# Eight PSUM banks, shared out anew while only attention runs: five for the scores and two for the transposes instead of three and four

## The chip, the cores and the metric

The kernel runs on one core of a Trainium2 chip. The core has a matrix engine (TensorE, PE in the rows below; its weight loads are shown apart as PEld), a vector engine (DVE), a scalar engine (ACT), a general engine (POOL) and a queue that only issues transfers (SP). Each engine works through its own list of instructions in the order in which it was emitted and waits where an operand or a buffer isn't ready. Matrix results go to PSUM, which has eight banks of 128 x 512 float32; DVE and ACT read them there. The metric is the device time of one execution in microseconds (us), as the median of several runs.

## What is computed

Attention with pooled queries, then two MLPs one after the other, on 4 batches, 8 heads, 1152 keys, 576 pooled queries and a head width of 64; then 2304 tokens with a model width of 512 and 2048 hidden units.

```python
q_pool = q.reshape(B, H, S // 2, 2, D).mean(axis=3)
scores = scale * np.matmul(q_pool, k.transpose(0, 1, 3, 2))
scores = scores - np.max(scores, axis=-1, keepdims=True)
attn = np.exp(scores)
attn = attn / (np.sum(attn, axis=-1, keepdims=True) + 1e-09)
x = heads_to_columns(np.matmul(attn, v))                  # [2304, 512]
h = x @ w_in;  x = np.maximum(0.01 * h, h) @ w_out        # first MLP
h = x @ w_in2; g = np.where(h > 0.0, h, np.exp(np.minimum(h, 0.0)) - 1.0)
out = g @ w_out2
```

## The kernel before

Every large product is carried in pieces: a float32 value is split into h (rounded) and l (the rest), and the product is the sum of three, or of two with h stacked over l.

Attention goes by pairs of heads: 4 batches of 4 pairs, 16 pairs in all. A pair has nine tiles of 128 queries. For one tile:

- `scores` (L438): three score matmul groups of 384 keys, each into a PSUM bank of its own (L452, two or four matmuls), the maximum of each bank on DVE (L457), the maximum of the three (L459, DVE), and then three exponentials on ACT (L463), which read the same three banks again and write P to SBUF. A score bank is free only after its exponential.
- `transpose_p` (L469): P goes through PE again in three groups of three 128 x 128 transposes, each group into a PSUM bank (L475). ACT copies the bank out as h (L261), DVE subtracts to get l (L267), and then the bank is free.
- `pv` (L489): P times V into the one bank `o` (L496), added up on ACT (L507) and DVE (L509).

Each pair also has transposes of its keys (`kn`) and queries (`qn`, `qxn`) into PSUM (L373), copied out by ACT (L386, L409, L418). At its end `normalise` (L513) transposes the reciprocal sums twice (L535, L542), and DVE multiplies out of these two banks (L538, L546). A pair ends with L538.

The MLPs take a batch at a time (L629 up, L667 down), and begin as soon as a batch's four pairs are normalised. So the first four pairs, those of batch 0, run with no MLP beside them; after that an MLP always does. What runs beside the first four pairs on DVE, ACT and POOL is the conversion of MLP weights (`ct`, `cr`, `cm`, `wr`, L293 to L305), as far as there are buffers for it.

The eight banks have names: three `s`, two `t`, one `o`, two `h`. `h` is the MLPs' pair. While the first four pairs are emitted (`first_window`), a table EARLY lends `h` to attention: `pbank` (L432) deals out the banks of a use in the order that the table's string spells.

The order of the instructions of each engine is made by a list scheduler in the kernel (`Program`, L37), from costs in the code, ranks, and the rule that a bank's next use waits for all readers of its last. A change of the banks therefore gives every engine another order.

Of the kernel before, what the change touches and what calls it, by code (L numbers as in the profile page):

```python
# [18 lines left out]
class Buf:  # L19
    """A tile that is allocated when the first operation on it is emitted."""  # L20
# [16 lines left out]
class Program:  # L37
    """Operations in the order of the computation, emitted in the order in which a
    list schedule by their costs (ns) and ranks starts them.

    A tile's k-th use of a tag waits for its (k - bufs)-th to be through."""
# [15 lines left out]
    def add(self, engine, cost, rank, fn, w=(), r=()):  # L57
        """fn() emits; w and r name the tiles (or (tile, part)) written and read."""
        me = len(self.ops)
        deps, starts, frees = set(), set(), []  # L60
# [4 lines left out]
        for x in r:  # L65
            b, part = x if isinstance(x, tuple) else (x, None)
# [88 lines left out]
def kernel(  # L155
# [11 lines left out]
    """Pooled-query attention, then a leaky-max MLP, then an ELU MLP.  # L167

    Every float32 operand of a large product is carried as h + l, h being the
    value rounded to float32r and l the exact rest (also a float32r); products  # L170
    sum h*h + h*l + l*h. Contractions of 64 stack h over l on 128 partitions.
    Tokens of a batch are kept in columns (t, p) -> row 4 p + t for the first
    512 and in order for the last 64; the output stores undo that.
    """
# [6 lines left out]
    NQ = S // 2  # L181
# [30 lines left out]
    EARLY = {'s': 'sss', 't': 'tthh'}  # L212
# [36 lines left out]
    def act(n, accum=False, sbuf=False):  # L249
        return 50 + 0.833 * n + (190 if accum else 0) + (43 if sbuf else 0)  # L250
# [7 lines left out]
    def psplit(rank, h, l, hi, lo, src, n, w, r, w_l=None, fast=True, psum=False):  # L258
        """hi = round(src) on engine h, lo = src - hi on engine l (AP makers)."""
# [11 lines left out]
    def convert(rank, dst, src):  # L271
        """dst = src, a [128, 512] block of weights, as float32; float64 comes as its bits.

        With e the 11 exponent bits, a float32's exponent is e's top bit and its
        low seven while 897 <= e <= 1150; below that the value is a zero. The
        mantissa's last 29 bits are rounded and added to the rest as integers.
        """
# [33 lines left out]
    def load_w(rank, layer, w_in, w_out, f):  # L311
        """h and l of the f-th 128 hidden units' columns of w_in and rows of w_out."""
# [456 lines left out]
```

## Time and profile before

| | us |
|---|---|
| median of 3 runs (lowest, highest) | 1550.54 (1548.72, 1550.97) |
| span of the profiled execution | 1550.8 |
| PE busy in it | 1421.8 (92%) |
| DVE busy | 1093.0 (70%) |
| ACT busy | 1027.4 (66%) |
| POOL busy | 844.7 (54%) |

The profiled execution's span is 0.3 us above the median of the runs and within their spread. Busy times are of the whole span; the stages differ much, so the rows below give them for stretches.

### The profile page before, as it was taken

How to read it: one execution, taken by the hardware profiler on the slowest of the kernel's cores; microseconds unless marked ns; L12 is line 12 of the kernel's file. 1: busy time of each engine (PE TensorE's matmuls, PEld its weight loads, DVE VectorE, ACT ScalarE, POOL GpSimd, SP SyncE). 2: the span in 40 equal slices, each digit the busy share in tenths (PEclk: the TensorE clock that was granted, in tenths of full speed). 3: DMA queues.
4: the chain of work that ended last, by engine and by line, in shares of the span. 5: the costliest groups of instructions: out<-in, count | busy, mean ns of one | idle time of the engine just before them, and what ended most of it. 6: DMA issues, size and time to landing. Idle time of an engine off the chain costs nothing.

```text
span 1550.8 us, 28885 instructions
## 1 busy us (share of the span) xinstructions
PE 1421.8 (92%) x10288; PEld 1368.2 (88%) x10288; DVE 1093.0 (70%) x2401; ACT 1027.4 (66%) x2773; POOL 844.7 (54%) x840
## 2 busy tenths in 40 slices
PE   5878899889888888999999999999999998899998
PEld 5777788878777788999999998999999998899897
DVE  6998898989999999656676767556676664224333
ACT  6998888777677777676667766776667652442442
POOL 5444256666666667444455556454554445566572
PEclk9999999999999999999999999999999999999999
DMA  4232124433334443222222222222221111322230
GB/s 145 90 114 86 40 79 139 128 114 124 125 119 136 142 133 115 83 77 60 69 74 70 79 77 63 93 73 61 70 71 42 55 55 56 92 76 82 69 89 31
DMA packets 82641, 135.58 MB, mean 87 GB/s; under 512 B 8512, under 2 KB 26944, under 8 KB 82496
## 3 DMA queue, kind: packets, MB, share of 16 engines
q1 hardware_dynamic: 82496, 133.73, 28.4%
q8 instruction: 81, 1.33, 0.4%
q14 instruction: 64, 0.52, 0.1%
HBM read 112.20 MB, written 21.50 MB: 86 GB/s over the span
## 4 chain that ended last, share of the span: by engine, by line
PE 50%; DVE 13%; ACT 3%; issue 2%; DMA 2%; POOL 2%; SPq 0%; ACTq 0%; POOLq 0%; DVEq 0%
PE h L667 15%; PE h L629 12%; PE s L452 5%; PE o L496 5%; PE t L475 4%; PE s L629 2%; DVE t L648 2%; PE s L667 2%; PE t L629 2%; DVE wr L305 2%; PE t L667 2%; DVE t L651 1%; PE t L373 1%; DVE pt L267 1%; DVE m L457 1%
## 5 line engine op out<-in xcount | busy, mean ns | idle before, releaser
L667 PE MATMUL h<-g,wo 128*128 128x288 f32 x2544 | 442.1, 305 | 18.5 <-DVE t L651 10.8
L629 PE MATMUL h<-xs,wi 128*128 128x288 f32 x2520 | 428.2, 305 | 22.9 <-DVE t L651 9.7
L629 PEld LDWEIGHTS h<-xs,wi 128*128 128x128 f32 x2520 | 362.8, 191 | 35.7 <-DVE t L651 15.4
L667 PEld LDWEIGHTS h<-g,wo 128*128 128x128 f32 x2544 | 368.6, 190 | 23.9 <-DVE t L651 13.0
L457 DVE TENSOR_REDUCE m<-s 128x1 f32<-128x384 f32 x432 | 231.3, 550 | 53.0 <-PE s L452 50.0
L267 POOL TENSOR_TENSOR g<-t,g 128x288 fp32r<-128x288 f32 x256 | 218.9, 863 | 89.3 <-ACT g L261 85.6
L261 ACT ACTIVATE pt<-t 128x384 fp32r<-128x384 f32 (+1 forms) x416 | 183.0, 455 | 126.1 <-PE t L475 116.4
L463 ACT ACTIVATE p<-s,m 128x384 f32<-128x384 f32 x432 | 248.4, 585 | 23.1 <-DVE m L459 22.7
L267 DVE TENSOR_TENSOR pt<-t,pt 128x384 fp32r<-128x384 f32 (+1 forms) x416 | 206.1, 508 | 56.6 <-ACT pt L261 55.0
L267 POOL TENSOR_TENSOR wo<-wr,wo 128x512 fp32r<-128x512 f32 x128 | 168.3, 1321 | 136.0 <-ACT wo L261 126.9
L452 PE MATMUL s<-kT,qT 128*128 128x384 f32 x768 | 195.2, 353 | 27.9 <-ACT p L463 27.6
L267 POOL TENSOR_TENSOR wi<-wr,wi 128x512 fp32r<-128x512 f32 x128 | 171.4, 1339 | 62.4 <-ACT wi L261 50.6
L475 PE MATMUL t<-ident,p 128*128 128x128 f32 x1116 | 181.1, 276 | 19.4 <-DVE pt L267 13.2
L496 PE MATMUL o<-pt,vn 128*128 128x256 f32 (+1 forms) x1152 | 190.7, 301 | 4.4 <-DVE pt L267 2.5
L496 PEld LDWEIGHTS o<-pt,vn 128*128 128x128 f32 x1152 | 164.4, 189 | 8.4 <-DVE pt L267 5.6
L261 ACT ACTIVATE g<-t 128x288 fp32r<-128x288 f32 x256 | 112.7, 446 | 88.1 <-DVE t L651 50.0
L475 PEld LDWEIGHTS t<-ident,p 128*128 128x128 f32 x1116 | 137.9, 142 | 31.5 <-DVE pt L267 14.1
L642 DVE SCALAR_TENSOR_TENSOR t<-t 128x288 f32<-128x288 f32 x128 | 90.6, 714 | 97.1 <-ACT t L640 96.6
L303 POOL TENSOR_TENSOR ct<-ct,cr 128x256 uint32<-128x256 uint32 x128 | 98.8, 773 | 109.5 <-DVE ct L296 41.0
L452 PEld LDWEIGHTS s<-kT,qT 128*128 128x128 f32 x768 | 126.1, 192 | 35.9 <-ACT p L463 34.5
L267 POOL TENSOR_TENSOR vn<-raw,vn 128x576 fp32r<-128x576 f32 x32 | 45.9, 1436 | 166.2 <-ACT vn L261 166.2
L261 ACT ACTIVATE wo<-wr 128x512 fp32r<-128x512 f32 x128 | 80.3, 630 | 83.0 <-PE h L667 51.8
(104 smaller groups left out, 2091.6 us busy)
## 6 DMA issues: line engine op xcount, KB each, us to landing
wr<-w SPq DMA_DIRECT2D x192, 256.0 KB, 2.7
cr<-in_moe_w_in_dram SPq DMA_DIRECT2D x64, 256.0 KB, 2.7
cr<-in_moe_w_out_dram SPq DMA_DIRECT2D x64, 256.0 KB, 2.7
w<-wr SPq DMA_DIRECT2D x64, 256.0 KB, 2.1
raw<-in_k_dram SPq DMA_DIRECT2D x32, 288.0 KB, 3.1
raw<-in_v_dram SPq DMA_DIRECT2D x32, 288.0 KB, 3.0
raw<-in_q_dram SPq DMA_DIRECT2D x32, 256.0 KB, 3.0
out_dram<-cr SPq DMA_DIRECT2D x16, 256.0 KB, 2.2
```

The lines of the kernel that those rows point to most:

```text
L261: prog.add("ACT", act(n, sbuf=not psum), rank, lambda: A.activation(out=hi(), in_=src(), func=ACTF.Copy), w=[w], r=r)
L267: lambda: eng.tensor_tensor(out=lo(), in0=src(), in1=f32(hi()), op=ALU.subtract),
L303: prog.add("POOL", pool(CW), rank, lambda t=t, r=r: G.tensor_tensor(out=t.ap, in0=t.ap, in1=r[:, :, 0], op=ALU.add), w=[t], r=[t, (r, 0)])
L305: prog.add("DVE", dve(CW), rank, lambda n=n, t=t, mag=mag: V.scalar_tensor_tensor(out=dst[:, n:n + CW], in0=mag.ap, scalar=MIN_HI, in1=t.a ...
L452: PE.matmul(out=st[:, 0:384], lhsT=qa(a), rhs=kT[:, 384 * c:384 * c + 384], start=(i == 0), stop=(i == len(seq) - 1))
L457: prog.add("DVE", dve(384), rank - LR, lambda st=st, c=c: V.tensor_reduce(out=m[:, c:c + 1], in_=st[:, 0:384], axis=AX.X, op=ALU.max), w=[ ...
L463: prog.add("ACT", act(384, True), rank - LE, lambda c=c: A.activation(out=p[:, 384 * c:384 * c + 384], in_=banks[c][:, 0:384], func=ACTF.E ...
L475: PE.transpose(out=t[:, i, :], in_=p[:, (3 * c + i) * 128:(3 * c + i + 1) * 128], identity=ident)
L496: PE.matmul(out=o[:, 0:n], lhsT=vn[:, c, :], rhs=pt[th][:, a, c % 3, :], start=(c == 3 * ORDER[0] and a == 0), stop=(c == 3 * ORDER[2] + 2 ...
L629: PE.matmul(out=h[:, 0:HB], lhsT=wi[:, a, c, :], rhs=xs[c][:, e, cols], start=(c == 0 and a == 0 and e == 0), stop=(c == DC - 1 and a == 1))
L642: prog.add("DVE", dve(HB), rk, lambda t=t, g32=g32: V.scalar_tensor_tensor(out=g32.ap, in0=t.ap, scalar=0.01, in1=t.ap, op0=ALU.mult, op1= ...
L667: PE.matmul(out=y[:, 0:HB], lhsT=w[f][1][:, a, d * 128:(d + 1) * 128], rhs=g[f][:, e, cols], start=(f % FC == 0 and a == 0 and e == 0), st ...
```

## The change

The table's two strings are exchanged in their sense: the scores rotate over five banks (three `s`, then two `h`), and all transposes, of P, of keys and queries and of the reciprocal sums, keep the two `t` alone. Nothing else in the code changes (the diff also drops docstrings and comments, which aren't shown).

```diff
     SBUFS = 3
     RAWB = 3
-    EARLY = {'s': 'sss', 't': 'tthh'}
+    EARLY = {'s': 'ssshh', 't': 'tt'}
     T1B = 3
     HBUFS = 2
```

How PE's order changes from the third pair to the fourth, beginning with the normalisation of the third (`rb`: its reciprocal sums, `p`: P of a tile, `kn` and `qn`: keys and queries of the fourth pair's second head; the bank is named ahead of the arrow). Before:

```order
L452 MATMUL s<-kT,qT 128x384 x6
L535 MATMUL h<-ident,rb 128x128 x4
L542 MATMUL t<-ident,rb 128x128
L475 MATMUL t<-ident,p 128x128 x3
L475 MATMUL h<-ident,p 128x128 x6
L452 MATMUL s<-kT,qT 128x384 x4
L373 MATMUL t<-identr,kn 128x128 x6
L373 MATMUL h<-identr,kn 128x128 x3
L452 MATMUL s<-kT,qT 128x384 x2
L373 MATMUL h<-identr,qn 128x128 x4
L373 MATMUL t<-identr,qn 128x128 x4
L475 MATMUL t<-ident,p 128x128 x3
```

After the change, at the same place:

```order
L535 MATMUL t<-ident,rb 128x128 x4
L542 MATMUL t<-ident,rb 128x128
L452 MATMUL s<-kT,qT 128x384 x4
L475 MATMUL t<-ident,p 128x128 x9
L373 MATMUL t<-identr,kn 128x128 x3
L452 MATMUL s<-kT,qT 128x384 x2
L373 MATMUL t<-identr,kn 128x128 x6
L373 MATMUL t<-identr,qn 128x128 x8
L475 MATMUL t<-ident,p 128x128 x9
```

Thirteen groups of transposes in a row (two of `rb`, three of `p`, three of `kn`, two of `qn`, three of `p`) now share two banks, where four took them in turn; six score matmuls stand among them in both.

PE's order inside the fourth pair, from the transposes of the tile that mixes two heads (its scores are those with `rem`). Before:

```order
L475 MATMUL t<-ident,p 128x128 x6
L475 MATMUL h<-ident,p 128x128 x3
L452 MATMUL s<-kT,qT 128x384 x2
L475 MATMUL h<-ident,p 128x128 x3
L452 MATMUL s<-kT,qT 128x384 x2
L475 MATMUL t<-ident,p 128x128 x3
L452 MATMUL s<-kT,qT 128x384 x2
L475 MATMUL t<-ident,p 128x128 x3
L496 MATMUL o<-pt,vn 128x320 x12
```

After:

```order
L475 MATMUL t<-ident,p 128x128 x6
L452 MATMUL s<-kT,qT 128x384 x4
L475 MATMUL t<-ident,p 128x128 x3
L452 MATMUL h<-kT,qT 128x384 x2
L475 MATMUL t<-ident,p 128x128 x3
L452 MATMUL h<-kT,qT 128x384 x2
L452 MATMUL s<-kT,qT 128x384 x2
L475 MATMUL t<-ident,p 128x128 x6
L452 MATMUL s<-kT,qT 128x384 x2
```

Six groups of scores, two tiles, now stand where three stood, and they have moved ahead of transposes that they followed.

DVE's order up to the end of the fourth pair (L538). Before:

```order
L457 TENSOR_REDUCE m<-s 128x1 x3
L509 TENSOR_TENSOR xu<-o,tm 64x256
L459 TENSOR_REDUCE m<-m 128x1
L538 TENSOR_TENSOR xu<-h,xu 128x512
L267 TENSOR_TENSOR pt<-t,pt 128x3x128
```

After:

```order
L457 TENSOR_REDUCE m<-s 128x1
L459 TENSOR_REDUCE m<-m 128x1
L457 TENSOR_REDUCE m<-s 128x1
L509 TENSOR_TENSOR xu<-o,tm 64x256
L457 TENSOR_REDUCE m<-s 128x1
L538 TENSOR_TENSOR xu<-t,xu 128x512
L457 TENSOR_REDUCE m<-s 128x1
```

Two maxima of the next tile have moved ahead of L538; counted over the whole list, 116 maxima stand ahead of it instead of 114, and at the ends of the three pairs before it 37, 64 and 91 instead of 33, 60 and 87. The weight conversions ahead of the third and the fourth L538 are the same number as before. On PE, 18 matmuls of the first MLP (L629) now stand ahead of the fourth L535, where there were none. From the 3621st PE instruction on, of 10290, the order of PE is that of before.

## Rows read from the trace of the kernel before

**Rows 1.** The page's first lines: span, then busy us, share of the span and instructions of each engine.

```profile
span 1550.8 us, 28885 instructions
PE 1421.8 (92%) x10288; PEld 1368.2 (88%) x10288; DVE 1093.0 (70%) x2401; ACT 1027.4 (66%) x2773; POOL 844.7 (54%) x840
```

**Rows 2.** The end of each of the first four pairs: the four instructions of L538 on DVE (start us, length us, what).

```profile
67.33 0.69 DVE L538 TENSOR_TENSOR xu<-h,xu 128x512 f32<-128x512 f32 x1
113.62 0.69 DVE L538 TENSOR_TENSOR xu<-h,xu 128x512 f32<-128x512 f32 x1
159.14 0.69 DVE L538 TENSOR_TENSOR xu<-h,xu 128x512 f32<-128x512 f32 x1
201.93 0.69 DVE L538 TENSOR_TENSOR xu<-h,xu 128x512 f32<-128x512 f32 x1
```

**Rows 3.** Busy time by stretch: the first four pairs, then the stretch up to 620 us, then the rest (stretch, its length, busy us and instructions of each engine, granted clock, DMA share, GB/s).

```profile
0.00:67.33 67.33, 45.43 (x289) 40.80 (x289) 53.62 (x127) 52.42 (x145) 33.23 (x42) 1.00 0.43 131
67.33:113.62 46.29, 37.27 (x254) 33.73 (x254) 43.16 (x107) 42.15 (x123) 21.27 (x23) 0.96 0.31 97
113.62:159.14 45.52, 37.11 (x254) 33.90 (x254) 40.54 (x102) 40.51 (x118) 18.54 (x19) 0.96 0.27 86
159.14:201.93 42.79, 35.77 (x257) 32.90 (x258) 35.81 (x86) 36.15 (x104) 12.04 (x13) 1.00 0.14 42
201.93:620.00 418.07, 363.45 (x2553) 339.60 (x2552) 390.31 (x842) 311.06 (x863) 273.64 (x283) 0.98 0.40 124
620.00:1551.00 931.00, 902.81 (x6685) 887.23 (x6683) 529.58 (x1138) 545.13 (x1423) 485.97 (x465) 0.99 0.24 70
```

**Rows 4.** Waits of PE, DVE and ACT from 0 to 201 us: who waited for what, us in total, times, longest.

```profile
PE s L452 <- ACT p L463: 28.6, 17, 4.6
PE h L475 <- DVE xu L538: 3.1, 3, 1.1
...
DVE m L457 <- PE s L452: 10.4, 18, 1.3
DVE ct L293 <- DMA cr<-in_moe_w_in_dram: 7.1, 5, 6.0
DVE qn L263 <- PE h L373: 3.5, 3, 1.7
...
ACT pt L261 <- PE t L475: 7.4, 14, 1.6
ACT p L463 <- DVE m L459: 6.0, 10, 1.3
```

**Rows 5.** The same view of DVE for the second and the fourth pair alone.

```profile
DVE m L457 <- PE s L452: 0.3, 1, 0.3
...
DVE m L457 <- PE s L452: 3.6, 8, 0.8
```

**Rows 6.** One tile of the fourth pair in order of time, PE, DVE and ACT (start us, length us, engine, line, what; in brackets the engine's idle time ahead of it and what ended that).

```profile
171.66 2.35 PE L452 MATMUL s<-kT,rem 128*128 128x384 f32 x12 [1.44 <-ACT p L463]
172.66 1.95 DVE L457 TENSOR_REDUCE m<-s 128x1 f32<-128x384 f32 x3 [0.37 <-PE s L452]
173.85 0.82 PE L475 MATMUL t<-ident,p 128*128 128x128 f32 x6
174.38 0.87 ACT L261 ACTIVATE pt<-t 128x384 fp32r<-128x384 f32 x2 [1.65 <-PE t L475]
174.72 0.15 DVE L459 TENSOR_REDUCE m<-m 128x1 f32<-128x3 f32 x1
174.90 1.02 DVE L267 TENSOR_TENSOR pt<-t,pt 128x384 fp32r<-128x384 f32 x2
175.13 0.50 ACT L261 ACTIVATE pt<-h 128x384 fp32r<-128x384 f32 x1
175.50 0.59 ACT L463 ACTIVATE p<-s,m 128x384 f32<-128x384 f32 x1
176.24 0.62 PE L452 MATMUL s<-kT,qT 128*128 128x384 f32 x2 [1.25 <-ACT p L463]
```

**Rows 7.** The passage from the third pair to the fourth in order of time: PE, ACT and DVE; and behind the dots another group of transposes of P and of keys with their copies.

```profile
157.49 0.60 PE L535 MATMUL h<-ident,rb 128*128 128x128 f32 x4
159.89 0.55 PE L475 MATMUL h<-ident,p 128*128 128x128 f32 x3 [1.04 <-DVE xu L538]
162.46 0.51 PE L373 MATMUL h<-identr,qn 128*128 128x128 f32 x4
163.00 0.60 ACT L409 ACTIVATE qT<-h 128x512 fp32r<-128x512 f32 x1 [0.26 <-PE h L373]
163.50 0.82 PE L475 MATMUL h<-ident,p 128*128 128x128 f32 x6
163.76 1.60 DVE L263 CAST xs<-xu 128x288 fp32r<-128x288 f32 x2
...
169.07 0.49 PE L475 MATMUL t<-ident,p 128*128 128x128 f32 x3
170.83 0.54 DVE L267 TENSOR_TENSOR pt<-t,pt 128x384 fp32r<-128x384 f32 x1
185.82 0.37 PE L373 MATMUL t<-identr,kn 128*128 128x128 f32 x3
186.23 0.49 ACT L386 ACTIVATE kT<-t 128x384 fp32r<-128x384 f32 x1
```

**Rows 8.** Waits of PE from 201 to 260 and from 260 to 620 us, where the transposes have two banks beside the MLPs.

```profile
PE t L475 <- DVE pt L267: 2.5, 5, 0.9
...
PE t L475 <- DVE pt L267: 10.5, 15, 1.9
```

## The prediction

> **What bounds the kernel now.** I read the busy time by stretch first, cut at the ends of the first four pairs [rows 2, 3]. Three stages show. Up to 201.93 us only attention runs, with weight conversions beside it. There no engine is full: idle is 67.33 - 53.62 = 13.7 us of DVE in the first pair, then 3.1, 5.0 and 7.0; of ACT 14.9, 4.1, 5.0 and 6.6; of PE 21.9, 9.0, 8.4 and 7.0. From 201.93 to 620 us DVE is the bound: idle 418.07 - 390.31 = 27.8 us (7%), PE 54.6. From 620 us on it is PE, busy 902.81 of 931 us (97%). The change touches the first stage alone, 13% of the span, so no more can come of it than that stage's idle time.
>
> Then the waits up to 201 us [rows 4]. PE stands 28.6 us, 17 times, in front of scores until an exponential has freed a bank. PE is not full, so that matters only as far as it passes on: DVE waits 10.4 us, 18 times, for scores to take a maximum of. That is the stall which five banks address. The other large waits of DVE are of another kind: 7.1 us for weights from DMA, 6.0 us of them one wait at the start, and 3.5 us for the bank transposes of queries that read its `qn` buffer.
>
> Last the order of time in one tile [rows 6]. The scores of a tile start at 171.66 us, the next tile's at 176.24: a period of 4.58 us. The three banks are read for the maxima until 174.61, the common maximum ends at 174.87, ACT still has copies of P's transposes to make, the exponential starts at 175.50 and ends at 176.09, and only then has the next tile a bank; DVE then has nothing to reduce. The wait is 1.25 us here, 1.44 one tile earlier. With five banks two of the next tile's three score groups needn't wait for this exponential.
>
> The Trainium skill, page "Perfetto Trace Analysis", section "Optimization Strategy", says that the same gap repeating on an engine may mean that there isn't enough PSUM for the next tile. The trace agrees on the gap, 1.25 and 1.44 us in two tiles that follow each other [rows 6]; whether banks alone are short there no row shows.
>
> **The change, part by part.** No instruction is added or removed; matmuls, maxima, exponentials, copies and transfers keep their counts and durations. What changes is which bank a group waits for, and the order.
>
> *Scores over five banks.* DVE's waits for scores, 10.4 us, can go at most. They aren't even: 0.3 us in the second pair, where conversions fill DVE, 3.6 us in the fourth, where few are left [rows 5]. The order bears out that scores run ahead: four more maxima stand ahead of the ends of the first three pairs, two more ahead of the fourth. Some of the waits will stay, because a score group that has a free bank can still stand behind a blocked transpose on PE. I take 2 us for that, by the longest that a transpose waits for its bank today where it has two (1.9 us, [rows 8]), and count -8.4 us. Bounds: 0 and -10.4; with the waits for `qn` gone too, which a shorter queue on PE could do, -13.9.
>
> *All transposes on two banks.* A group of P holds its bank from PE's start to the end of DVE's subtraction: 173.85 to about 175.44 (half of the pair that ends at 175.92), 1.6 us at best, and 169.07 to 171.37, 2.3 us, in another tile [rows 6, 7]. A group of keys holds it from 185.82 to 186.72, 0.9 us; one of queries from 162.46 to 163.60, 1.1 us [rows 7]. A pair has 27 groups of P, 6 of keys, 4 of queries, 1 of the rest and 2 of sums. On two banks that is at least (27 x 1.6 + 13 x 1.1) / 2 = 29 us and with 2.3 us for P 38 us, beside a pair of 42.8 to 46.3 us [rows 2]. So on average two banks do, but not by much; they are short where transposes stand close.
>
> That is where one pair passes into the next. There 13 groups now stand in a row on two banks. Along one bank: the sums 157.49 to 159.89, 2.4 us [rows 7]; two groups of P at 1.6 to 2.3; keys 0.9; queries 1.1; then the first P group of the second tile starts 7.6 to 9.0 us after L535, and that tile's third group, on the same bank, 9.2 to 11.3. Before, the group at 163.50 is followed at once by the tile's last, 6.4 us after L535. So PE is 2.8 to 4.9 us later at each passage. How much of it reaches DVE isn't in the trace. DVE has other work there: four maxima have been done ahead, but 1.6 us of casts for the MLP [rows 7] and conversions, while there are any, can be done meanwhile. The lower bound is 0 and the upper 4.9; I take 1.5, nearer to the lower one, since the deeper score queue lets the following tiles make up for some. Three passages lie within the stage (at 67, 114 and 159 us): +4.5 us, bounds 0 and 14.7. A fourth, at 202 us, has MLP work beside it and counts nothing; without that cover it would be another 1.5.
>
> *Outside the table.* The first MLP's 18 matmuls that are now ahead of the fourth L535 move PE work (nothing on PE is the bound before 620 us), 0. Conversions ahead of the third and fourth end of a pair are as many as before, so DVE's work up to there is the same but for two maxima, and a gain at 202 us isn't paid back in conversions. DVE's other 27.8 us of idle up to 620 us stay by my count; a new order there may move them, and a quarter, 7 us, is as much as I'd put to it, in either direction. After that the order is the same, and a stage bound by PE starts as much earlier as the one ahead of it ends.
>
> **Sum.** -8.4 + 4.5 = -3.9 us on the execution's 1550.8 us [rows 1]: 1546.9. The median of the runs is 0.3 us lower: 1546.6 us.
>
> **The rivals.**
>
> *It is taken back by the transposes (no change).* Each passage costs about 2.8 us instead of 1.5: -8.4 + 8.4 = 0, 1550.5 us. For it: ACT's largest wait already today is for transposes, 7.4 us [rows 4], and it has four banks now. Against it: the tiles between passages need only 3 groups each, 3 x 2.3 / 2 = 3.5 us, within their period of 4.58 us.
>
> *The transposes become the bound (slower).* Place: the passages. From 2.8 us of DVE stall each they decide; at the full 4.9 us they cost 14.7 and the end is -8.4 + 14.7 = +6.3, 1556.8 us. For it: where the transposes have only two banks today PE does wait for them, 2.5 us between 201 and 260 us and 10.5 us up to 620 us [rows 8], and not at all up to 201 us except 3.1 us behind L538 [rows 4]. Against it: those 20 waits are 0.65 us in the mean, and DVE is 93% busy there all the same [rows 3].
>
> The Trainium skill, page "Perfetto Trace Analysis", section "Matmuls", asks that independent groups rotate through different PSUM banks, so that their evacuation overlaps the next group. For the scores that speaks for the change, for the transposes, which go from four banks to two, against it; which of the two weighs more it doesn't say.
>
> *The score waits weren't the bound at all.* DVE and ACT have about equal idle in each pair [rows 3], and ACT's waits for the maximum are 6.0 us [rows 4]; if the exponentials and copies on ACT set the pace, DVE's wait only changes its name. Then the sum is 0 less what passages cost: 1550.5 to 1555 us (three times 1.5).
>
> *More than that.* All 10.4 and 3.5 us go and the passages are hidden: 1550.5 - 13.9 = 1536.6 us.
>
> **Chances.** The runs of before spread over 2.3 us, so 0.2%, 3.1 us, is about what a measurement tells from no change. My own case, including that of more, gets 0.46 for a gain over that; its own range is 1538 to 1547.4. Cases near zero (passages of 1.8 to 3.8 us, or scores that weren't the bound) 0.31; the slower ones 0.23. For 8 in 10: from 1539, most of the bound of -13.9, to 1556, where the slower rival is nearly whole.
>
> **What would show it.** Right: the waits of DVE for scores before the fourth L538 fall from 10.4 us to 2 or 3, PE's waits for exponentials from 28.6 us to under 10, and the fourth L538 starts at about 198 us. New waits of PE for `t` banks behind DVE's subtraction or L538 show at the passages, and the fourth L538 and the end of the span move by the same amount. Wrong: the fourth L538 is at 202 us or later, with ACT or DVE waiting for transposes as long as they waited for scores; or it is earlier and DVE's idle time from there to 620 us has grown by as much.

## The result: 1.5% slower, all of it lost in the first four pairs

The changed kernel takes 1574.36 us (median; 1571.43 to 1577.99), the kernel before 1550.67 in the same comparison: a ratio of 1.0148, 95% interval 1.0128 to 1.0168, or 23.7 us more. The forecast was 1546.6 us, and its range ended at 1556.

The page of the changed kernel, its first lines (columns as in [rows 1]):

```profile
span 1574.6 us, 28886 instructions
...
PE 1441.6 (92%) x10288; PEld 1374.9 (87%) x10288; DVE 1094.2 (69%) x2401; ACT 1031.7 (66%) x2773; POOL 844.3 (54%) x840
```

Busy time of the changed kernel by stretch, cut at its own four L538, which start at 73.12, 123.99, 177.27 and 226.84 us (columns as in [rows 3]):

```profile
0.00:73.12 73.12, 51.74 (x293) 42.73 (x293) 55.63 (x136) 55.18 (x154) 35.63 (x44) 0.95 0.39 124
73.12:123.99 50.87, 41.28 (x254) 34.53 (x254) 44.02 (x112) 43.09 (x124) 21.96 (x24) 0.90 0.31 97
123.99:177.27 53.28, 43.37 (x254) 37.23 (x254) 40.84 (x98) 39.47 (x112) 14.91 (x16) 0.84 0.20 60
177.27:226.84 49.57, 41.81 (x268) 35.64 (x268) 34.54 (x84) 36.64 (x104) 11.25 (x13) 0.93 0.13 37
226.84:644.00 417.16, 360.72 (x2538) 337.60 (x2538) 388.37 (x839) 311.22 (x858) 272.44 (x281) 0.98 0.39 123
644.00:1575.00 931.00, 902.66 (x6682) 887.12 (x6682) 530.80 (x1139) 546.08 (x1423) 488.07 (x467) 0.99 0.24 70
```

Against [rows 2, 3] the four pairs are 5.8, 4.6, 7.8 and 6.8 us longer, 24.9 in all. Work on DVE and ACT hardly grew: DVE has 175.0 us busy in the four, 173.1 before, and ACT 174.4 for 171.2. What grew is DVE's idle time, from 28.8 to 51.8 us. PE's busy time grew as well, from 155.6 to 178.2 us; it holds 18 matmuls of the first MLP and matmuls at a lower clock, to which the third experiment comes. Everything behind the fourth L538 takes 1347.8 us, 1348.9 before. So the loss stands in the stage that the change touches, in each pair, the first included, which has no passage from another pair in it.

The waits of the changed kernel from 0 to 227 us (us in total, times, longest), and under it the one row of the kernel before, up to 202 us, that [rows 4] doesn't hold:

```profile
ACT pt L261 <- PE t L475: 29.3, 38, 2.8
...
PE t L475 <- DVE pt L267: 17.3, 22, 2.4
...
DVE pt L267 <- ACT pt L261: 14.3, 25, 2.3
...
PE s L452 <- ACT p L463: 7.2, 15, 1.6
...
DVE m L457 <- PE s L452: 5.4, 9, 1.6
...
DVE m L457 <- PE h L452: 2.4, 6, 0.5
...
PE h L452 <- ACT p L463: 2.0, 5, 0.7
```

```profile
DVE pt L267 <- ACT pt L261: 0.5, 1, 0.5
```

PE's waits for exponentials fell from 28.6 to 7.2 + 2.0 = 9.2 us (the second figure is for scores in the `h` banks), and DVE's for scores from 10.4 to 5.4 + 2.4 = 7.8. In their place stands a ring of three that was hardly there: ACT waits for a transpose (before 7.4 [rows 4], and 1.4 more for those in the `h` banks), DVE's subtraction waits for ACT's copy (0.5), and PE's next transpose waits for that subtraction, which frees the bank (before there is no such wait in this stage). These waits aren't bound to the passages: of PE's 17.3 us for subtractions only 0.8, 0.4 and 0.5 fall in the 10 us behind the first three L538.

The passage from the third pair to the fourth in the changed kernel, PE's transposes in order of time (the same place as [rows 7]; in brackets PE's idle time and what ended it):

```profile
175.36 0.60 PE L535 MATMUL t<-ident,rb 128*128 128x128 f32 x4
...
178.10 0.52 PE L475 MATMUL t<-ident,p 128*128 128x128 f32 x3 [1.32 <-DVE xu L538]
...
179.98 0.55 PE L475 MATMUL t<-ident,p 128*128 128x128 f32 x3 [0.54 <-DVE pt L267]
...
184.95 0.90 PE L475 MATMUL t<-ident,p 128*128 128x128 f32 x3 [0.18 <-ACT qT L409]
...
186.01 1.92 PE L475 MATMUL t<-ident,p 128*128 128x128 f32 x6 [0.15 <-ACT qT L409]
...
187.03 0.50 PEld L475 LDWEIGHTS t<-ident,p 128*128 128x128 f32 x3 [0.52 <-DVE pt L267]
```

```profile
176.00:180.00 4.00, 1.83 (x12) 1.08 (x10) 3.75 (x11) 1.03 (x3) 2.21 (x3) 1.00 0.26 66
180.00:184.00 4.00, 3.02 (x18) 2.39 (x18) 1.83 (x4) 3.33 (x10) 0.74 (x1) 0.74 0.03 10
184.00:188.00 4.00, 3.54 (x18) 2.56 (x17) 1.51 (x3) 2.91 (x8) 2.63 (x2) 0.50 0.00 0
```

The second tile's three groups of P begin at 184.95, 186.01 and 187.03, where the weights of the third are loaded after a wait for a subtraction. That is 11.7 us behind L535, a little over the upper end of the walk (9.2 to 11.3); before it was 6.4. The lower fence is busy time by stretch at the same place: PE has 1.83 of 4 us to do, and then a granted clock of 0.74 and 0.50, the 1.2 GHz level. A group that takes 0.52 us at 178.10 takes 0.90 at 184.95.

### The profile page after: what moved, and what is told of

Read it like the earlier page. It is cut to its first block, busy times and chain, and to the rows that moved or that the text cites. A ratio compares the mean times of both kernels' runs of the same rounds, so it can differ in the third digit from the quotient of the medians.

```text
span 1574.6 us, 28886 instructions
## 1 busy us (share of the span) xinstructions
PE 1441.6 (92%) x10288; PEld 1374.9 (87%) x10288; DVE 1094.2 (69%) x2401; ACT 1031.7 (66%) x2773; POOL 844.3 (54%) x840
## 4 chain that ended last, share of the span: by engine, by line
PE 52%; DVE 18%; ACT 4%; issue 3%; DMA 3%; POOL 2%; ACTq 0%; POOLq 0%; SPq 0%; DVEq 0%
PE h L667 15%; PE h L629 13%; PE s L452 5%; PE o L496 5%; PE t L475 4%; PE s L629 2%; DVE t L648 2%; PE s L667 2%; DVE wr L305 2%; DVE m L457 2%; PE t L667 2%; PE t L629 2%; DVE ct L296 2%; DVE pt L267 2%; DVE t L642 2%
## 5 line engine op out<-in xcount | busy, mean ns | idle before, releaser
L629 PE MATMUL h<-xs,wi 128*128 128x288 f32 x2520 | 427.4, 304 | 22.7 <-DVE t L651 11.7
L629 PEld LDWEIGHTS h<-xs,wi 128*128 128x128 f32 x2520 | 361.6, 190 | 34.9 <-DVE t L651 19.4
L261 ACT ACTIVATE pt<-t 128x384 fp32r<-128x384 f32 (+1 forms) x480 | 211.4, 459 | 148.3 <-PE t L475 141.8
L267 DVE TENSOR_TENSOR pt<-t,pt 128x384 fp32r<-128x384 f32 (+1 forms) x480 | 238.4, 511 | 73.0 <-ACT pt L261 70.2
L475 PE MATMUL t<-ident,p 128*128 128x128 f32 x1296 | 217.5, 283 | 36.1 <-DVE pt L267 26.2
L457 DVE TENSOR_REDUCE m<-s 128x1 f32<-128x384 f32 x390 | 210.0, 550 | 47.8 <-PE s L452 45.4
L463 ACT ACTIVATE p<-s,m 128x384 f32<-128x384 f32 x390 | 224.9, 585 | 18.3 <-DVE m L459 17.9
L475 PEld LDWEIGHTS t<-ident,p 128*128 128x128 f32 x1296 | 160.7, 144 | 60.6 <-DVE pt L267 30.7
L452 PE MATMUL s<-kT,qT 128*128 128x384 f32 x696 | 180.7, 358 | 18.8 <-ACT p L463 17.6
L496 PE MATMUL o<-pt,vn 128*128 128x256 f32 (+1 forms) x1152 | 194.3, 305 | 2.7 <-DVE pt L267 2.7
L496 PEld LDWEIGHTS o<-pt,vn 128*128 128x128 f32 x1152 | 168.5, 194 | 4.1 <-DVE pt L267 4.0
L452 PEld LDWEIGHTS s<-kT,qT 128*128 128x128 f32 x696 | 115.4, 194 | 28.9 <-ACT p L463 26.4
```

The source lines that it names most:

```text
L261: prog.add("ACT", act(n, sbuf=not psum), rank, lambda: A.activation(out=hi(), in_=src(), func=ACTF.Copy), w=[w], r=r)
L267: lambda: eng.tensor_tensor(out=lo(), in0=src(), in1=f32(hi()), op=ALU.subtract),
L452: PE.matmul(out=st[:, 0:384], lhsT=qa(a), rhs=kT[:, 384 * c:384 * c + 384], start=(i == 0), stop=(i == len(seq) - 1))
L457: prog.add("DVE", dve(384), rank - LR, lambda st=st, c=c: V.tensor_reduce(out=m[:, c:c + 1], in_=st[:, 0:384], axis=AX.X, op=ALU.max), w=[ ...
L463: prog.add("ACT", act(384, True), rank - LE, lambda c=c: A.activation(out=p[:, 384 * c:384 * c + 384], in_=banks[c][:, 0:384], func=ACTF.E ...
L475: PE.transpose(out=t[:, i, :], in_=p[:, (3 * c + i) * 128:(3 * c + i + 1) * 128], identity=ident)
```

## The experiments

Kernels are named by the banks that the first four pairs have: s for the scores, t for the transposes. Before is 3 and 4, the change 5 and 2. Ratios are to the kernel before on the same chip.

**First: which half of the exchange costs.** Three banks for scores, as before, and two for transposes, run twice; then three and three; then four and two; and four and three, where one bank of the four is dealt to both uses in turn.

```diff
-    EARLY = {'s': 'ssshh', 't': 'tt'}
+    EARLY = {'s': 'sss', 't': 'tt'}
+    EARLY = {'s': 'sss', 't': 'tth'}
+    EARLY = {'s': 'sssh', 't': 'tt'}
+    EARLY = {'s': 'sssh', 't': 'tth'}
```

> The transposes have two banks as in the changed kernel, but the scores keep their three (the two banks of the MLPs lie idle while only attention runs). Theory A, the two-bank round trip of the transposes costs the time: at least as slow as the changed kernel, 1572 to 1585 us, ends of the first four pairs at 73 us and then 50 us or more apart. Theory B, it is the scores that run ahead on five banks and push the subtractions of the transposes back on DVE: near the kernel before, 1550 to 1557 us. Theory C, the low granted clock costs the time: slow where PE has long pauses; the granted clock of the first 227 us at or under the 0.90 of the changed kernel, and the time goes with the clock.

> The banks of the first four pairs: three for the scores, as before, and three for the transposes, t, t and h in turn; the fourth h stays unused. A point between the kernel before (three and four, 1551.6 us) and three and two (1561.8). If the transposes' banks are what the time hangs on, by the number of them: about 1554 to 1557 us, with ACT's waits for transposes before the fourth L538 between 8.8 and 18.6 us. If two is a cliff (a pair of banks can't hold one group while it is copied and another while it is subtracted, three can): within 2 us of before, 1550 to 1553.

> Four banks for the scores and two for the transposes, one bank of the MLPs idle. Theory A, only the two t banks count: the same as with three score banks, 1559 to 1565 us. Theory B, every score bank more costs: halfway, 1566 to 1570 us.

> One bank given back: the scores rotate over four, the transposes over three. Theory A: the transposes' round trip needs more than two banks, so most of the loss goes: 1546 to 1555 us. Theory B: the scores still run ahead by one bank, about half the loss stays: 1558 to 1566 us. Theory C: the granted clock of the first 200 us is back at 0.97 to 1.00 and the time near 1550 us.

| scores and transposes | us | ratio, 95% interval |
|---|---|---|
| 3 and 3 | 1555.39 | 1.0027 (1.0014 to 1.0040) |
| 3 and 2 | 1561.79 | 1.0065 (1.0041 to 1.0088) |
| 4 and 2 | 1573.76 | 1.0163 (1.0122 to 1.0203) |
| 4 and 3, one shared | 1574.99 | 1.0150 (1.0122 to 1.0177) |
| 5 and 2, the change | 1574.36 | 1.0148 (1.0128 to 1.0168) |

Fewer banks for transposes cost by degrees, some 4 us for the first taken and 6 for the second. More banks for scores gain nothing back: the fourth costs another 12 us (by the medians) and the fifth nothing more. A bank dealt in turn to both uses didn't help as a third bank for the transposes. Each of these kernels has its own order on every engine as well as its own banks, so the table doesn't say which of the two costs; the fifth part takes them apart. Waits of the first run of three and two from 0 to 216 us:

```profile
ACT pt L261 <- PE t L475: 18.6, 30, 1.7
PE s L452 <- ACT p L463: 14.9, 18, 2.5
...
DVE m L457 <- PE s L452: 13.2, 29, 1.6
...
PE t L475 <- DVE pt L267: 8.9, 16, 0.8
```

**Second: the passages.** The prediction put the cost there. In the changed kernel, the sums' transposes, which hold a bank until L538, go to the bank `o`; and in a second kernel those of keys and queries too (the edit of `tr_r`), so that only P's are left on the two banks.

```diff
     def normalise(rank, b, hp):
-        t = pbank("t")
+        t = pbank("o" if first_window[0] else "t")
...
-        t2 = pbank("t")
+        t2 = pbank("o" if first_window[0] else "t")
     def tr_r(rank, src, get, n):
-        t = pbank("t", F32R)
+        t = pbank("o" if first_window[0] else "t", F32R)
```

> The changed kernel, but the two transposes of the reciprocal sums go into the bank o in the first four pairs, so that the transposes of P needn't wait for L538 there. If the stall at the passages is what costs (my prediction's slower rival): the pairs shorten by 2 to 4 us each and the time falls to 1560 to 1566 us. If the two banks are short all along the pair: 1570 to 1575 us.

> Five and two as in the change, but the transposes of keys, queries and sums of the first four pairs go into the bank of the products with V; only P's 27 groups of a pair use the two banks. By the prediction's own step (the passages, where 13 groups of all kinds stand in a row) this should undo most of the loss: 1555 to 1562 us. If P's groups along the whole pair are the bound: no better than 1570. The one bank of the products becomes busier, which can cost by itself.

The first takes 1578.04 us (1.0169, 1.0136 to 1.0203), no better than the change. That speaks against the 1.32 us behind L538 as what the stage waits for, but the lists of all engines differ too. The second takes 1570.55 us (1.0125, 1.0105 to 1.0145), 4 us better by the medians, with an interval that overlaps that of the change, and far from the 1555 to 1562 of the prediction's step. But its trace reads otherwise. Its busy time by stretch:

```profile
0.00:210.83 210.83, 165.04 (x1068) 143.19 (x1068) 175.18 (x423) 171.76 (x489) 84.86 (x94) 0.97 0.30 90
210.83:645.00 434.17, 371.77 (x2569) 347.17 (x2570) 400.47 (x851) 312.66 (x865) 273.25 (x285) 0.97 0.38 120
```

The fourth L538 stands at 210.83 us, 16.0 earlier than in the change, and 12 of these are lost behind it: from there to the end of its span of 1570.8 it takes 1360.0 us, against 1347.8. The end of a stage tells nothing of the total when the order behind it changes as well; the last part comes back to that.

**Third: the granted clock.** The changed kernel has 0.84 to 0.95 in the four pairs where before had 0.96 to 1.00 [rows 3], so perhaps PE's pauses cost it the clock, and the clock the time. Three kernels give PE more to do at the same places: score matmuls issued twice in three tiles of a pair, the second score group of every tile issued twice, and 16 score matmuls into the bank `o` at each passage.

```diff
-            def mm(st=st, c=c):
-                for i, (_, qa, a, kT) in enumerate(seq):
+            def mm(st=st, c=c, reps=2 if first and idx in (2, 4, 6) else 1):
+                for i, (_, qa, a, kT) in reps * list(enumerate(seq)):
...
+            def mm(st=st, c=c, reps=2 if first and c == 1 else 1):
...
+                for i in range((8, 4, 4)[c] if fill else 0):
+                    PE.matmul(out=o[:, 0:384], lhsT=fill[0][:, 0, 0, :], rhs=fill[1][:, 0:384], start=True, stop=True)
```

> The changed kernel's banks and its order on every engine; the score matmuls of the second to fourth tile of each of the first four pairs are issued twice into the same bank, so the result is the same and PE has some 3.6 us more work in each of these pairs, most of it where one pair passes into the next. Theory A: PE's extra work stands in the chain of the transposes, so the time is that of the changed kernel or longer, 1574 to 1585 us, whatever the clock. Theory C: the fuller PE keeps the granted clock up (0.96 or more over the first four pairs instead of 0.90) and the time falls, in spite of the extra work, to 1555 to 1565 us.

> As the run before it, but the extra matmuls are spread: the second of the three score groups of each tile in the first four pairs is issued twice, some 3.6 us of PE in each pair as well. Theory A: 1574 to 1590 us. Theory C: the same amount of extra work away from the pauses holds the clock less well: between the changed kernel and the run before it, 1560 to 1572 us, with a granted clock of 0.92 to 0.96.

> The changed kernel with the same order on every engine, but where the first pair passes into the second, the second into the third and the third into the fourth, PE issues 16 score matmuls more, into the bank o that nothing reads then (8 ahead of the first transposes of P of the new pair, 4 ahead of each of the next two groups), so that PE has no pause there in front of the two t banks. Nothing that is read changes. Theory C, the low granted clock behind these pauses is a large part of the loss: the granted clock of pairs two to four rises from 0.90, 0.84 and 0.93 to 0.97 or more, and they get shorter by 3 to 6 us each: 1559 to 1566 us. Theory A, the two banks' round trips set the time whatever the clock: 1573 to 1582 us, also where the clock is back at 1.00.

1580.23 us (1.0183, 1.0158 to 1.0208), 1581.34 (1.0191, 1.0169 to 1.0213) and 1572.79 (1.0143, 1.0128 to 1.0158). Up to the fourth L538 they have a granted clock of 0.93, 0.92 and 0.93, the change 0.91: none held the clock up, so none can say what the clock is worth. Busy time by stretch around the third passage of the last one:

```profile
174.00:178.00 4.00, 4.00 (x27) 3.69 (x26) 3.42 (x10) 1.53 (x3) 1.42 (x1) 1.00 0.13 17
180.00:184.00 4.00, 2.83 (x22) 2.30 (x22) 1.70 (x4) 4.00 (x13) 0.38 (x1) 0.98 0.00 2
184.00:190.00 6.00, 5.56 (x26) 4.88 (x25) 2.60 (x5) 3.52 (x11) 3.71 (x5) 0.50 0.16 44
```

PE is full through the filled stretch at the full clock, pauses for 1.2 of 4 us while ACT works without a gap, and has 0.50, the 1.2 GHz level, in the stretch behind. What the clock is worth came from another place: the two runs of three and two are one program, and their profiled executions differ in the clock of the first two pairs alone.

> Three banks for scores and two for transposes once more, for a narrower figure: 1561.8 us before, ratio 1.0065. Five score banks in the same order gave 1.0054 [1.0037, 1.0071]. If the score banks' waits bound anything here, this ratio should be clearly above that, 1.008 or more; if they don't, between 1.004 and 1.007.

It took 1562.81 us (1.0075, 1.0051 to 1.0098). First and second pair of the first run, then of the second:

```profile
0.00:71.14 71.14, 49.96 (x283) 41.27 (x283) 55.13 (x134) 54.95 (x151) 36.10 (x45) 0.95 0.42 135
71.14:123.21 52.07, 42.03 (x260) 35.84 (x260) 47.81 (x115) 44.39 (x126) 23.59 (x25) 0.90 0.31 99
```

```profile
0.00:69.04 69.04, 48.46 (x283) 39.62 (x283) 55.02 (x133) 55.18 (x151) 36.14 (x45) 0.98 0.44 139
69.04:120.44 51.40, 39.99 (x260) 34.05 (x260) 47.36 (x114) 44.33 (x126) 23.64 (x25) 0.97 0.31 99
```

A clock of 0.95 over 71.14 us is 2 x 0.05 x 71.14 = 7.1 us at half speed; with the second pair, 17.5 us in the first run and 5.9 in the second. The pairs are 2.1 and 0.7 us longer, the two behind them equal within 0.04: 2.8 us for 11.6, or 0.24 us for each us at half speed. The changed kernel has 41 us at half speed in the four pairs, the kernel before 7. By this one pair of executions, an estimate from clocks given to two places, some 8 of the 24.9 us go by way of the clock. I take it for a price on PE's pauses and no cause of its own; no run here changes the clock and leaves the order, but for this pair.

**Fourth: scores that run too far ahead.** Counted in PE's order, the scores stand 3.7 groups ahead of the P group that is transposed next in the kernel before, 4.7 with three and two, 6.6 with four and two, 6.9 with the change. That goes with the times, but for four and three with the shared bank (3.7 groups, 1575 us). So the ranks of scores and maxima were put later in the first four pairs; then the same ranks with the banks of before and with three and two; and last, instead, copies and subtractions were ranked earlier.

```diff
-            prog.add("PE", 163 * len(seq), rank - LS, mm, w=[st], r=reads)
+            prog.add("PE", 163 * len(seq), rank - (0.9 if first_window[0] else LS), mm, w=[st], r=reads)
...
-        prog.add("DVE", 70, rank - LR, lambda: V.tensor_reduce(
+        prog.add("DVE", 70, rank - (0.5 if first_window[0] else LR), lambda: V.tensor_reduce(
...
+            rk = rank - (2.5 if first_window[0] else 0)
...
-                psplit(rank, "ACT", "DVE", hi, lambda hi=hi: hi(1), lambda t=t, s0=s0, n=n: t[:, 0:3, s0:s0 + n],
+                psplit(rk, "ACT", "DVE", hi, lambda hi=hi: hi(1), lambda t=t, s0=s0, n=n: t[:, 0:3, s0:s0 + n],
```

The last three lines are of the last kernel alone, whose score ranks are the old ones.

> The changed kernel's banks, but while only attention runs the scores and their maxima get a rank that doesn't put them ahead of the transposes and subtractions of the tile before (the leads 2.5 and 2 become 0.9 and 0.5 tiles), so the five banks fill no further ahead than three did. Theory B, scores that run ahead hold up the subtractions that free the t banks: back to the level of three score banks with two t banks, 1558 to 1565 us. Theory A: no change, 1570 to 1577 us.

> The banks of before (three and four) with the ranks of scores and maxima put later in the first four pairs, as in the run that took five and two from 1574.4 to 1565.6 us. A control: if those 8.7 us came because scores no longer ran ahead over the five banks, before has little to gain from it, since its three banks hold scores back anyway: 1549 to 1555 us. If later scores are simply the better order whatever the banks, it should gain as much, 1543 to 1546 us, and the gain there says nothing on running ahead.

> Three banks for scores, two for transposes, with the later ranks. If five score banks do their harm by letting scores run ahead, then with later ranks three and five score banks should come out alike, both near 1562 to 1566 us (three with early ranks: 1561.8; five with later ranks: 1565.6). If the ranks help in themselves, it falls to about 1553 us.

> Five and two as in the change, but in the first four pairs the copies and subtractions that free a transposes' bank get a rank 2.5 tiles earlier, so that the scheduler puts them level with the scores of the tile that runs ahead. If late subtractions are the cause, PE's waits for them (17.3 us in the changed kernel) and ACT's for transposes (29.3) fall and the time goes to 1560 to 1566 us. If the two banks are short whatever the order, 1572 to 1576.

| banks, ranks | us | ratio, 95% interval | groups ahead |
|---|---|---|---|
| 5 and 2, later scores | 1565.64 | 1.0089 (1.0067 to 1.0111) | 5.5 |
| 3 and 4, later scores | 1596.69 | 1.0304 (1.0285 to 1.0323) | 1.9 |
| 3 and 2, later scores | 1589.61 | 1.0257 (1.0240 to 1.0273) | 3.1 |
| 5 and 2, earlier subtractions | 1576.93 | 1.0164 (1.0134 to 1.0194) | 6.9 |

Less ahead helps the change by 9 us, and its clock in the four pairs is no better (0.98, 0.87, 0.86, 0.89). But it hurts three score banks by 28 to 45 us, and three and two didn't come out level with five and two, as running ahead alone would have it. Earlier ranks for the subtractions change next to nothing: up to the fourth L538 PE's and ACT's lists stay as they were and DVE's has two pairs of neighbours exchanged. The scheduler had the subtractions where it could, so this run is hardly more than a repeat of the change and doesn't test earlier subtractions. So the distance ahead isn't the cause by itself; the order as a whole matters, and by tens of us.

**Fifth: the order against the banks.** The change does two things at once. It gives the chip other banks to wait for, and it gives the scheduler other rules, from which every engine's list comes. Two kernels part them. Both have the order that the scheduler makes for three and two up to the fourth L538 (but for some of the first MLP's matmuls on PE and a few neighbours exchanged on DVE and ACT); on the chip one has five and two, the other the three and four of before. In the first, a score group waits in the plan, beside what it waits for on the chip, for the third before it; in the second, a group of transposes waits in the plan for the second before it.

```diff
+            if first_window[0]:
+                st.plan = held[-3] if len(held) >= 3 else None
+                held.append(st)
...
+            if b.plan is not None:
+                frees.append(b.plan)
...
+    SEEM = dict(s=3, t=2)
+            h = held.setdefault(use, [])
+            b.prev = h[-SEEM[use]] if len(h) >= SEEM[use] else None
+            b.before = h[-1] if h else None
+            h.append(b)
```

> Five banks for the scores and two for the transposes as in the change, but the scheduler plans as if a score group had to wait for the one three before it: the order on every engine is that of three score banks and two (1561.8 us) but for some MLP matmuls on PE, and only the waits on the chip are those of five banks. If the order that five banks make the scheduler write is what costs the other 12.6 us, this comes out at 1561.8 or a little below (1557 to 1562), with PE's waits of scores for exponentials small. If it is the banks or the clock that PE's new pauses bring, whatever the order: 1570 to 1575 us.

> The banks of before, three and four, but the scheduler plans as if a transposes' group had to wait for the second before it: up to the fourth L538 the order on DVE, ACT and, but for MLP matmuls, PE is that of three and two (1561.8 us, fourth L538 at 216.2). If the two banks themselves cost the 10 us, four banks in this order end the fourth pair at about 202 to 206 us and the whole near 1551. If it is the order, the fourth L538 stays at 212 to 216 and the whole at 1557 to 1562. Order and waits after the fourth pair differ a little, so the fourth L538 is the reading, the total only with up to 10 us of doubt.

Five and two in that order takes 1558.60 us (1.0054, 1.0037 to 1.0071), 16 us less than the change, with the same banks. Its stretches up to the fourth L538, and its waits up to there (lines stand a few further down, since lines were added: L480 is the transposes of P, L269 the subtraction, L263 the copy, L462 and L457 maxima and scores):

```profile
0.00:70.28 70.28, 50.61 (x285) 42.18 (x285) 55.43 (x133) 54.54 (x151) 36.37 (x45) 0.95 0.44 137
70.28:121.32 51.04, 39.34 (x254) 33.47 (x254) 47.60 (x115) 44.33 (x126) 23.63 (x25) 0.93 0.32 100
121.32:167.66 46.34, 37.95 (x254) 32.85 (x254) 36.33 (x89) 36.83 (x107) 11.50 (x12) 0.96 0.20 54
167.66:214.09 46.43, 38.73 (x270) 33.96 (x270) 35.32 (x87) 36.20 (x105) 12.01 (x12) 1.00 0.14 39
```

```profile
PE t L480 <- DVE pt L269: 18.3, 30, 1.5
...
DVE pt L269 <- ACT pt L263: 7.7, 22, 0.7
DVE m L462 <- PE s L457: 6.8, 12, 1.0
...
DVE m L462 <- PE h L457: 4.1, 7, 1.0
```

PE's waits of scores for exponentials are gone (14.9 us with three score banks). In their place PE waits longer at the transposes, 18.3 us for 8.9.

Three and four in that order takes 1566.00 us (1.0096, 1.0075 to 1.0117), slower in all than five and two, but its order behind the fourth L538 is another one. Up to there (L470 is the exponentials, L464 and L459 maxima and scores; copy and subtraction have their old lines):

```profile
0.00:70.25 70.25, 47.20 (x283) 41.72 (x283) 55.62 (x133) 55.35 (x151) 35.98 (x45) 0.95 0.44 137
70.25:120.77 50.52, 39.67 (x254) 34.95 (x254) 47.02 (x115) 43.89 (x126) 23.61 (x25) 0.93 0.32 99
120.77:165.91 45.14, 38.71 (x254) 34.02 (x254) 35.98 (x89) 37.05 (x107) 11.48 (x12) 0.96 0.20 57
165.91:210.93 45.02, 38.31 (x260) 33.36 (x261) 34.81 (x86) 36.44 (x105) 12.00 (x12) 1.00 0.14 40
```

```profile
PE s L459 <- ACT p L470: 29.8, 26, 3.3
...
DVE m L464 <- PE s L459: 9.6, 22, 1.0
...
DVE pt L267 <- ACT pt L261: 6.5, 18, 0.7
```

Its fourth L538 lies between the two readings that were expected, 202 to 206 us for the banks and 212 to 216 for the order, so each has a share in what three and two lose. Its total lies above both ranges that were expected.

The fourth L538, step by step:

| order planned for | banks on the chip | fourth L538 at | step |
|---|---|---|---|
| 3 and 4 | 3 and 4 (before) | 201.93 us | |
| 3 and 2 | 3 and 4 | 210.93 us | order +9.0 |
| 3 and 2 | 5 and 2 | 214.09 us | banks +3.2 |
| 5 and 2 | 5 and 2 (the change) | 226.84 us | order +12.8 |

Along this path the order is 21.8 of the 24.9 us and the banks are 3.2. Three and two itself, in the same order and at the same clock up to there (0.96), stands at 216.15 us: the two transposes' banks that are taken away cost 5.2 us, and the two score banks that are added give 2.1 back. Each is one profiled execution, and one program gave 213.39 and 216.15 us (three and two, the former at a clock of 0.98), so single steps are good to some 3 us. That the order is the larger part isn't in doubt: by the medians the change and five and two in the other order, with the same banks, are 16 us apart. The order's part includes what goes by way of the clock, which is 0.98 up to the fourth L538 in the first row, 0.96 in the next two and 0.91 in the last. DVE's wait for ACT's copy shows the order at work: 6.5 us, 18 times, with the four banks of before and only another order, where it was 0.5 us, once. In this order DVE comes to subtractions before their copies are done, also with four banks; whether DVE's list has them too early or PE's and ACT's lists bring the copies too late isn't shown.

The order of before with only two banks for the transposes wasn't tried: its lists would stand still, each engine waiting for another. So the banks' price is known in one order alone, and the split of the 24.9 us for this path alone.

**Sixth: a better version, and the order behind the fourth pair.** The same edits as in the second part, with the banks of before.

> The banks of before, but in the first four pairs the two groups of transposes of the reciprocal sums go into the bank of the products with V instead of one of the transposes' four. In the kernel before PE waits 3.1 us, three times, behind L538 with a P group. If that wait costs time, this gains up to 3 us: 1548 to 1549 us. If it is covered, as the same edit at two banks showed no gain (1578.0), 1550 to 1553 us.

> The banks of before (three and four), with the transposes of keys, queries and sums of the first four pairs in the bank of the products with V. The sums alone there gave 1542.5 us against 1551.6. If that gain is less crowding on the transposes' banks, this gives as much or a little more, 1539 to 1543. If it is an order that happened to fall well after the fourth pair, it can go either way, 1543 to 1556, and the fourth L538 tells nothing of the total.

The sums' transposes alone in `o`: 1542.47 us, 0.9946 (0.9927 to 0.9964), by the ratio 8 us faster than the kernel before and the best of all. Those of keys and queries there too: 1551.73 us, 1.0000 (0.9988 to 1.0013). Busy time by stretch of the faster one:

```profile
0.00:203.46 203.46, 157.45 (x1066) 143.12 (x1067) 175.19 (x424) 171.99 (x491) 85.28 (x94) 0.98 0.30 94
203.46:620.00 416.54, 367.58 (x2596) 342.55 (x2595) 396.10 (x856) 314.31 (x869) 275.82 (x285) 0.99 0.39 125
```

Its fourth L538 is 1.5 us later than before. It gains behind it: DVE idles 416.54 - 396.10 = 20.4 us up to 620, against 27.8 [rows 3], and from the fourth L538 to the end of the span of 1542.4 it takes 1338.9 us, 10.0 less. So what was gained isn't the 3.1 us of waits behind L538 but another order in a stretch that the edit doesn't name. Over the kernels here that remainder goes from 1338.5 us (the slower of these two: its span is 1551.0, its fourth L538 at 212.54) to 1360.0 (the second of the second part).

## Why the prediction was wrong, step by step

**What bounds the kernel.** Right as far as it went: the first stage alone changes, no engine is full there, and the remainder stays (1347.8 us for 1348.9). That it stays was no law, though; the same stretch moved by 21 us between kernels, three times the 7 us that the prediction allowed for a new order and then left out of its range.

**Scores over five banks, -8.4 us.** The mechanism half holds. PE's waits for exponentials went as forecast (28.6 to 9.2 us and, in the order of three and two, from 29.8 with three and four banks to no row with five and two). DVE's waits for scores were to go with them, from 10.4 to 2 or 3, and didn't: 7.8 in the change, and in one order 9.6 with three score banks and 6.8 + 4.1 = 10.9 with five. In that order the total with five score banks is 1.0054 and with three 1.0065 and 1.0075, intervals that overlap: 2 or 3 us, as the 2.1 us at the fourth L538 have it, not 8.4. A score group was late because of a bank; when the bank was there, PE stood at the transposes ahead of it in its list instead (8.9 us of waits for subtractions with three score banks, 18.3 with five). The sentence that the prediction takes from the Trainium skill, page "Perfetto Trace Analysis", section "Optimization Strategy", leaves out that the page speaks of gaps on the engine that should be saturated; PE, busy 155.6 of 201.9 us [rows 3], isn't that here.

**All transposes on two banks, +4.5 us.** The size was right and the place at best half right. In one order two banks instead of four move the fourth L538 from 210.93 to 213.39 or 216.15, 2.5 to 5.2 us; the walk through the passage came out at 11.7, over its upper end. But in that order the four pairs of three and two (first run) are 0.9, 1.55, 1.2 and 1.55 us longer than with four banks, the first too, which has no passage from another pair in it; and in the change nine tenths of PE's waits for subtractions lie away from the passages. The argument that between passages 3 groups x 2.3 / 2 = 3.5 us fit into a period of 4.58 counts a bank's mean time; the waits of PE, ACT and DVE for each other don't appear in it. For the prediction's place speaks the kernel with only P's groups on the two banks, whose fourth L538 came 16.0 us earlier; but its order is another one as well.

**The order, 0 us.** This is the step that failed. The prediction read the new order as a sign that scores run ahead, and so of the gain, and priced the rest of it at nothing inside the pairs. It is 21.8 of the 24.9 us along the path above; with 5.2 for the transposes' banks and -2.1 for the scores' that is the whole. The scheduler works by costs written in the code and the new rules on banks, and the list that it made for two banks is 9 us worse than that for four even when the chip has the four, and the list for five and two another 12.8 worse than that for three and two. What in the lists does it is settled only in part. Seen are the subtractions that wait for copies. Counted in PE's order are 31 P groups that stand alone, 5 twos and 22 threes before; 54, 14 and 8 for three and two; 34, 24 and 8 for five and two. Later ranks, with scores less far ahead, took 9 us off the change and cost 28 and 45 us with three score banks, so running ahead fails as a rule. How each of these turns into time stays open.

**The rivals.** The slower one, transposes as the bound, had the right sign and the right waits, but a quarter of the size (+6.3 us), and it too put all of it in the passages. That the score waits weren't the bound at all was right for its one term: in one order DVE's waits for scores didn't fall. None of the rivals had the order. The Trainium skill, page "Perfetto Trace Analysis", section "Matmuls", asks for independent groups to rotate through different banks; in one order the runs agree for the transposes, where two banks taken away cost 5.2 us up to the fourth L538, and show for two more score banks 2.1 us, which is within the doubt of a single execution.

**What would show it.** The marks were good: the fourth L538 at 202 or later, with ACT waiting for transposes as long as others had for scores, was the stated sign of failure, and it is what came, 226.84 us and 29.3.

## What to carry to other kernels

A change of buffers under a list scheduler is two changes, what the chip waits for and the order that the planner writes; price the second on its own, by planning with the old numbers on the new buffers or the other way round, before any wait is counted as gained. A wait that ends last on one engine (PE for a bank) needn't be what makes the next engine wait (DVE for scores); if the resource is given and that engine's waits stay, look for what stands ahead of it in the same list. And the end of the touched stage isn't the verdict: with another order the untouched stage behind it moved by up to 21 us here, once to a gain of 8 us over the kernel before.

## What the runs showed of the hardware

The granted clock fell to its lower level, 1.2 GHz, in this mixed work after stretches in which PE paused. In the changed kernel it is 0.50 from 184 to 188 us, behind four us with PE busy 1.83 and four with 3.02. In the last of the filled kernels it is 0.50 from 184 to 190 us behind a stretch with PE busy 2.83 of 4 us, although PE was full and at 1.00 from 174 to 178. One program had 5.9 and 17.5 us at half speed in two executions, and took 2.8 us more for the latter up to the fourth L538. That is about a quarter of the time at half speed, an estimate from this one pair; PE isn't full there (49.96 of 71.14 us in the first pair).
